# Weights cast by their own transfers from GpSimd's queue, in a kernel of chunked linear attention and a gated MLP

## The chip, the cores and the metric

The kernel runs on one core of a Trainium2 chip. The metric is the device time of one execution in microseconds (us); smaller is better. Times of before are the median of three runs.

A core has five engines that work side by side and meet at semaphores: TensorE (PE, matrix products; its weight loads are shown as PEld), VectorE (DVE), ScalarE (ACT), GpSimd (POOL) and SyncE (SP, which here only issues transfers). Data come from DRAM through 16 DMA engines into SBUF. Matrix products end in PSUM, here eight banks of 512 float32 a partition, used in pairs as tiles of two banks.

## The reference

A linear attention with a forget gate for every key channel runs over 768 steps, for 4 batches and 8 heads of 48 channels. Its output, as 3072 tokens of 384, goes through a layer whose activation is h times cos h.

```python
f = 1.0 / (1.0 + np.exp(-f_logit))
for t in range(S):
    state = f[:, :, t, :, None] * state + einsum('bhd,bhe->bhde', k[:, :, t], v[:, :, t])
    y[:, :, t] = einsum('bhd,bhde->bhe', q[:, :, t], state)
...
x = y.transpose(0, 2, 1, 3).reshape(B * S, H * D)
h = x @ w_in            # (3072, 384) @ (384, 2048)
g = h * np.cos(h)
out = g @ w_out         # (3072, 2048) @ (2048, 384)
```

All inputs and the output are float32. The kernel computes its products in bfloat16.

## The kernel before

**Tiling.** The sequence is cut into 24 chunks of 128 steps (4 batches of 6). Within a chunk the recurrence becomes matrix products: the logarithms of the gates are summed along the chunk by a product with a triangular matrix (`decay`), q and k are multiplied with the exponentials of these sums (the "qk" operations), scores are formed and masked ("sc", "am"), the state is moved on to the next chunk ("ps", "st", "sz" in `move_state`), and the chunk's output y is built from scores and state ("y"). It is turned into xT, tokens along the free axis, on PE or by a transposing transfer. The first 12 chunks are worked in pairs (`DUAL`, function `attend2`), in which a transfer reads two neighbouring rows of 192 bytes at once; the other 12 alone (`attend`).

**Decay.** `decay` runs for two chunks at a time: load f_logit, exp, ln, sum on PE, and two exponentials of the sum with either sign. Exp and ln use one ScalarE table, the cosine another; a change of table is a row ACT_TABLE_LOAD. Two such blocks make a group (`GROUPS`), whose exponentials stay together. `PR["gate"]` says for a group after how many cosines its first exponential may come. For the pairs in `HALVED` the loads of f, q and k, and the exponentials, are done in two halves of four heads, so that work can begin on the first.

**The MLP.** `moe` takes units of 128, 128 and then eleven times 256 tokens. A product h goes into a PSUM tile of two banks, each half from another stretch of w_in (L907, six products for 256 tokens, twelve for 128). ScalarE takes the cosine (L915), DVE multiplies (L924, into gT), and PE multiplies gT with w_out in four parts of four products for each 128 tokens (L934). One of DVE and ACT copies the result out (L513), and SP stores it (L942).

**Weights.** w_in and w_out are 3.1 MB each in float32. They come in four quarters each (`load_weights`). A quarter is 768 KB: SP's queue brings it as float32 into one of the six gT buffers, seen as float32, and then POOL, DVE or ACT casts it into `w_in_bf` or `w_out_bf` (L485). All products of L907 and L934 read from there.

**The order.** It is not written by hand. Every piece of work is entered in a planner (`Plan`) with its possible engines, their cost in ns, what it reads and writes, and a priority. `Plan.run` simulates the engines, picks at each step the operation that can start first (among those within `WINDOW`, that of the smallest priority), and thereby fixes the order of every engine's instructions and the buffers used. `PR` holds the priorities, `PIN` ties single operations to one engine. The planner's model of transfers is one bus: each takes its `dma` time after the one before it. `FETCH` belongs to a model of the instruction fetch of PE, and is 0 before. Where PE would stand still for long in the first 36 us of the plan, `keep_warm` puts in products with zeros (L448), whose results nobody reads.

**Dependencies inside a tile.** An operation that writes a whole `Val` waits for its last writer. A `Part` of a `Val` has writers of its own; a reader of the whole waits for all parts.

## Time and profile before

| what | value |
|---|---|
| median of 3 runs | 186.5 us (186.28 to 186.93) |
| profiled execution, its own time | 189.2 us |
| its span | 187.4 us |
| granted TensorE clock | 1.00 |
| products of w_in (L907), x624 | 67.9 us busy |
| products of w_out (L934), x400 | 68.9 us busy |
| cosines (L915, ACT), x48 | 53.4 us busy, 1113 ns each |
| gating products (L924, DVE), x48 | 60.1 us busy, 1265 ns each |
| casts of weights on POOL (L485), 4 | 1467 ns each |
| SP's queue, packets' time as a share of 16 engines' span | 78.4% |
| read from DRAM / written | 25.17 MB / 4.72 MB |

A row of instructions gives the line, engine, operation, output<-input by the program's names, shapes, count, busy time and the mean duration of one; behind the bar at the end stands the idle time of the engine just before them, and who ended it. In the slices of the span, each digit is a busy share in tenths. The chain of waits is followed back from the last instruction: each piece was released by the piece above it. "SPq" is time in which SP's queue issues a transfer, which is not the transfer itself. Times of a transfer "to landing" run from its issue until its data are there. PE's matmuls overlap, so that a row's mean (264 ns) is longer than the distance between two of them.

### The profile page before, as it was taken

The numbers are of one execution on the slowest core, as the hardware profiler recorded it, in microseconds if no ns is written. First come the engines' busy times: TensorE is split into PE (matmuls) and PEld (weight loads), VectorE is DVE, ScalarE is ACT, GpSimd is POOL, SyncE is SP. The second block draws the span as 40 slices with busy tenths as digits, with TensorE's granted clock in tenths as the row PEclk, the third lists the DMA queues.
The fourth block names the chain that finished last, engine by engine and source line by source line (L and its number), as shares of the span: only waits on it lengthen the run. The fifth ranks groups of instructions, "written<-read, shape, count | busy, mean of one in ns | idle before, by whom it ended". The sixth has DMA issues, their size and how long they took to land.

```text
span 187.4 us, 5205 instructions
## 1 busy us (share of the span) xinstructions
PE 177.6 (95%) x2169; PEld 129.9 (69%) x2169; DVE 130.3 (70%) x168; ACT 124.5 (66%) x156; POOL 69.6 (37%) x103
## 2 busy tenths in 40 slices
PE   6889789999989999999999999999999999999993
PEld 2456488767768785677776778876676976788663
DVE  5387888927669997538697577894588793477620
ACT  5585178897897599983779958699665720645401
POOL 8307274423544764431515724811681231000000
PEclk9999999999999999999999999999999999999999
DMA  5999999999999999999999989997884313111022
GB/s 140 272 259 315 379 380 348 229 235 302 251 181 215 245 181 204 190 240 186 184 218 189 128 220 189 222 199 138 203 170 82 63 25 84 42 45 42 2 85 84
DMA packets 99783, 34.51 MB, mean 184 GB/s; under 512 B 92976, under 2 KB 98224, under 8 KB 99760
## 3 DMA queue, kind: packets, MB, share of 16 engines
q1 hardware_dynamic: 99760, 34.19, 78.4%
q8 instruction: 17, 0.28, 0.7%
q14 instruction: 6, 0.05, 0.1%
HBM read 25.17 MB, written 4.72 MB: 159 GB/s over the span
## 4 chain that ended last, share of the span: by engine, by line
PE 68%; DMA 11%; SPq 8%; ACT 3%; POOL 3%; issue 3%; DVE 2%; DVEq 0%; POOLq 0%
PE ps L907 30%; PE ps L934 28%; SPq L499 6%; DMA gT<-in_moe_w_in_dram 6%; DMA ld<-in_q_dram 4%; SPq L479 2%; DMA xT<-yb 2%; POOL qk L642 2%; PE ps L831 2%; PE ps L863 1%; PE ps L569 1%; PE ps L859 1%; PE ps L845 1%; ACT f L537 1%; PE ps L626 1%
## 5 line engine op out<-in xcount | busy, mean ns | idle before, releaser
L924 DVE TENSOR_TENSOR gT<-ps,cosh 128x1024 bf16<-128x1024 f32 x48 | 60.1, 1265 | 16.7 <-ACT cosh L915 13.1
L915 ACT ACTIVATE cosh<-ps,halfpi 128x1024 bf16<-128x1024 f32 x48 | 53.4, 1113 | 24.4 <-PE ps L907 23.9
L907 PE MATMUL ps<-xT,w_in_bf 128*128 128x256 bf16 (+1 forms) x624 | 67.9, 264 | 1.5 <-DVE xT L513 0.4
L934 PE MATMUL ps<-w_out_bf,gT 128*128 128x384 bf16 (+2 forms) x400 | 68.9, 320 | 0.0
L907 PEld LDWEIGHTS <-w_in_bf 128*128 128x128 bf16 x624 | 56.1, 98 | 10.1 <-issue 1.7
L934 PEld LDWEIGHTS <-gT 128*128 128x128 bf16 x400 | 36.2, 98 | 20.3
L603 POOL TENSOR_TENSOR sz<-st,b 64x192 bf16<-64x192 f32 x32 | 16.8, 524 | 27.9 <-DVE st L596 24.9
L800 POOL TENSOR_TENSOR qk<-ld,b 128x384 bf16<-128x384 f32 x12 | 12.0, 1001 | 18.2 <-issue 6.4
L513 ACT COPY ot<-ps 128x384 f32<-128x384 f32 (+2 forms) x14 | 6.4, 454 | 17.7 <-PE ps L934 17.4
L835 DVE TENSOR_TENSOR am<-ps,umask 128x1024 bf16<-128x1024 f32 x12 | 14.5, 1216 | 3.7 <-PE ps L831 3.3
L698 DVE TENSOR_TENSOR am<-ps,pmask 128x1024 bf16<-128x1024 f32 x12 | 14.2, 1218 | 2.4 <-PE ps L693 1.9
L800 POOL TENSOR_TENSOR qk<-ld,bi 128x384 bf16<-128x384 f32 x12 | 11.9, 1002 | 6.2 <-DMA ld<-in_k_dram 6.1
L513 DVE COPY ot<-ps 128x384 f32<-128x384 f32 x11 | 6.1, 553 | 11.4 <-PE ps L934 11.4
L537 ACT ACTIVATE f<-f 128x768 f32<-128x768 f32 (+1 forms) x14 | 10.3, 748 | 3.6 <-DMA f<-in_f_logit_dram 3.6
L578 ACT ACTIVATE b<-ps 128x776 f32<-128x776 f32 (+1 forms) x14 | 10.1, 724 | 2.0 <-PE ps L566 1.6
L642 POOL TENSOR_TENSOR qk<-ld,b 128x384 bf16<-128x384 f32 x6 | 6.3, 1066 | 13.6 <-ACT b L578 11.7
L448 PE MATMUL ps<-zeros 128*128 128x512 bf16 x34 | 10.3, 430 | 1.0 <-DVE halfpi L375 1.0
L549 ACT ACTIVATE sp<-f 128x768 bf16<-128x768 f32 (+1 forms) x14 | 10.4, 751 | 0.3
L513 DVE CAST yb<-ps 128x384 bf16<-128x384 f32 x13 | 7.0, 552 | 4.7 <-PE ps L743 1.9
L578 ACT ACTIVATE bi<-ps 128x768 f32<-128x768 f32 (+1 forms) x14 | 10.1, 723 | 0.0
L513 ACT CAST yb<-ps 128x384 bf16<-128x384 f32 x9 | 4.3, 475 | 7.9 <-PE ps L743 6.1
L596 DVE TENSOR_TENSOR st<-ps,sz 128x384 f32<-128x384 f32 x16 | 8.8, 551 | 0.8 <-PE ps L845 0.7
(82 smaller groups left out, 177.3 us busy)
## 6 DMA issues: line engine op xcount, KB each, us to landing
out_dram<-ot SPq DMA_DIRECT2D x23, 192.0 KB, 2.8
f<-in_f_logit_dram SPq DMA_DIRECT2D x16, 192.0 KB, 4.3
ld<-in_q_dram SPq DMA_DIRECT2D x16, 192.0 KB, 4.3
ld<-in_k_dram SPq DMA_DIRECT2D x16, 192.0 KB, 3.8
gT<-in_moe_w_in_dram SPq DMA_DIRECT2D x4, 768.0 KB, 9.4
gT<-in_moe_w_out_dram SPq DMA_DIRECT2D x4, 768.0 KB, 11.5
ld<-in_v_dram SPq DMA_DIRECT2D x6, 384.0 KB, 5.7
ld<-in_v_dram SPq DMA_DIRECT2D x12, 192.0 KB, 3.7
```

What stands on the lines that cost most here:

```text
L499: P.op(nm + str(n), {"SP": 470.0}, lambda e, i=i, w=w, dst=dst: nc.sync.dma_start(out=(dst.ap if m == 2 else flat(dst.ap)).rearrange("p (h ...
L513: (nc.scalar.copy if e == "ACT" else nc.vector.tensor_copy)(out=o, in_=i_)
L537: first = P.op("exp", {"ACT": act(384 * w, "S")}, lambda e, s=s: nc.scalar.activation(out=flat(ft.ap[:, s]), in_=flat(ft.ap[:, s]), func=A ...
L578: nc.scalar.activation(out=out_.ap[:, s, :], in_=pc.ap.rearrange("p (m n) -> p m n", m=w)[:, :, 0:n], func=AF.Exp, scale=sign)
L603: eng().tensor_mul(out=like(S_out.ap, pv())[s, ..., r, :], in0=srcap()[s, ..., r, :], in1=d[..., None].broadcast_to(list(d.shape) + [D]))
L698: P.op("am", {"DVE": dve(1024)}, lambda e, sc=sc, am=am: nc.vector.tensor_mul(out=am.ap.rearrange("p r a n -> p (r a n)").rearrange("p (a ...
L800: P.op("qk", {"POOL": 1020.0}, lambda e, j=j, src=src, dec=dec: E(e).tensor_mul(out=qkv()[:, j, :, 0:D], in0=HB(src.ap), in1=HB(dec.ap[:, ...
L835: P.op("am", {"DVE": dve(1024)}, lambda e: nc.vector.tensor_mul(out=am.ap.rearrange("p r a n -> p (r a) n"), in0=sc.ap.rearrange("p (a n) ...
L907: nc.tensor.matmul(ph.ap[:, g * T:(g + 1) * T], lhsT=w_in_bf[:, f0 // 512, m, f0 % 512:f0 % 512 + 128], rhs=x[:, m, :], start=(g % (G // 2 ...
L915: nc.scalar.activation(out=co.ap, in_=ph.ap, func=AF.Sin, bias=halfpi),
L924: nc.vector.tensor_mul(out=o, in0=i0, in1=i1)
L934: nc.tensor.matmul(po.ap[:, 0:z - a], lhsT=gT.ap[:, j, i * C:(i + 1) * C], rhs=w_out_bf[:, j, a:z], start=(j == 0), stop=(j == KF - 1))
```

## The change

A quarter of the weights is now one transfer from GpSimd's queue, straight into `w_in_bf` or `w_out_bf`, which casts from float32 to bfloat16 on its way. The eight casts of L485 for weights are gone, and the stay in a gT buffer. In the planner such a transfer has a time before which it isn't placed (`hold`, in us, from `PR["wt"]`), costs 780 ns of POOL and reaches the bus 2400 ns later; the 800 ns that the planner added when the bus changed to weights are gone.

The two halves of a product h write parts of their tile, so that neither waits for the other in the plan. The four parts of an output product do the same, and whichever comes first in the order starts the sum in its bank, whichever comes last ends it.

The second pair of chunks (2 and 3) is no longer loaded and exponentiated in halves. `FETCH` is 6000 ns, the rule for filling products is a little wider, and the order is planned anew: all of `PR` and `PIN` are new values.

```diff
@@ -111,7 +111,7 @@
 
 class Op:
     __slots__ = ("seq", "eng", "fn", "prio", "table", "deps", "vals", "alloc", "start", "end",
-                 "lat", "waiting", "after", "grp", "dma", "name", "prior", "cost", "made", "form", "count")
+                 "lat", "waiting", "after", "grp", "dma", "name", "prior", "cost", "made", "form", "count", "hold")
 
 
 class Plan:
@@ -122,7 +122,7 @@
     FORM = 96.0
     WARM = 1000.0, 36000.0
     SPARE = 300.0
-    BLOCK, LEAD, FETCH = 256, 187, 0.0
+    BLOCK, LEAD, FETCH = 256, 187, 6000.0
     TABLE = 1290.0
     WINDOW = 120.0
 
@@ -130,12 +130,12 @@
         self.ops = []
 
     def op(self, name, eng, fn, reads=(), writes=(), prio=0.0, table=None, lat=0.0, grp=None,
-           dma=None, form=("full", "full"), count=0):
+           dma=None, form=("full", "full"), count=0, hold=0.0):
         o = Op()
         if PIN.get(len(self.ops)) in eng:
             eng = {PIN[len(self.ops)]: eng[PIN[len(self.ops)]]}
         o.name, o.eng, o.fn, o.prio, o.table = name, eng, fn, prio, table
-        o.lat, o.grp, o.dma, o.prior, o.form, o.count = lat, grp, dma, [], form, count
+        o.lat, o.grp, o.dma, o.prior, o.form, o.count, o.hold = lat, grp, dma, [], form, count, hold
         o.seq, o.deps, o.alloc, o.vals, o.after = len(self.ops), set(), [], [], []
         for v in reads:
             o.deps.update(v.writers)
@@ -161,7 +161,7 @@
     def run(self):
         free = {"PE": 0.0, "ACT": 800.0, "DVE": 3500.0, "POOL": 4500.0, "SP": 750.0}
         table, lock, bus, hot, pe_end, form, sent = None, None, 0.0, 0.0, 0.0, "full", []
-        warm, row = [], False
+        warm = []
         done, asked, due = 0, {}, self.LEAD
 
         def fetched(s, cost, count):
@@ -186,7 +186,7 @@
         while len(order) < n:
             cand = []
             for o in ready:
-                at, pe = 0.0, "PE" in o.eng
+                at, pe = o.hold * 1000.0, "PE" in o.eng
                 for d in o.deps:
                     t = d.end + (0.0 if pe and d.eng == "PE" else self.SEM)
                     if pe and d.eng == "PE":
@@ -239,8 +239,9 @@
                         for i in range(v.slot, v.slot + v.pool.size)}
                 idle = [(b["free"][i], i) for i in range(len(b["free"]))
                         if i in own - used or not (b["held"][i] or i in used)]
-                if idle and min(idle)[0] + 200.0 < t0:
-                    warm.append((o, t0, s - self.SPARE - t0, min(idle)[1]))
+                if idle and max(min(idle)[0] + 200.0, t0) + 300.0 < s - self.SPARE:
+                    at = max(min(idle)[0] + 200.0, t0)
+                    warm.append((o, at, s - self.SPARE - at, min(idle)[1]))
                 fetched(t0, s - self.SPARE - t0, int((s - self.SPARE - t0) / (427.0 if t0 < 3000.0 else 215.0)))
                 hot = 1.0 - (1.0 - hot) * math.exp((t0 - s + self.SPARE) / 2500.0)
                 pe_end = s - self.SPARE
@@ -254,14 +255,12 @@
             o.start = s
             free[e] = s + cost
             if o.dma is not None:
-
-                weights = o.name[0] == "w"
-                bus = max(s + cost + 700.0, bus) + o.dma + (800.0 if weights and not row else 0.0)
-                row = weights
+                bus = max(s + cost + (700.0 if e == "SP" else 2400.0), bus) + o.dma
                 o.end = bus + (1250.0 if len(sent) > 1 else 700.0)
-                sent.append(bus)
-                if len(sent) > 3:
-                    free[e] = max(free[e], sent[-4] + 900.0)
+                if e == "SP":
+                    sent.append(bus)
+                    if len(sent) > 3:
+                        free[e] = max(free[e], sent[-4] + 900.0)
             else:
                 o.end = s + cost + (self.PE_LAT if e == "PE" else 55.0 if e in ("ACT", "DVE") else 0.0)
                 o.lat = o.end - s - cost
@@ -308,44 +307,44 @@
 UNITS = [128, 128] + [256] * 11
 DUAL = [0, 2, 4, 6, 8, 10]
 FREE_GROUPS = 1
-HALVED = [0, 2]
+HALVED = [0]
 COLUMNS = [0]
 TURN_Y = range(14, 23)
 TURN_QK = range(10, 23)
 PR = {
 ...
-    "w_in": [-39.88, -40.08, -39.64, -38.03],
-    "w_out": [-34.2, -33.96, -37.04, -33.75],
-    "wc": [-70.63, -33.41, 50, 25.03, -16.34, 18.34, -16.44, -221.86],
-    "gate": [None, 2, 4, 12, 20, 24],
 ...
+    "w_in": [-12.77, -158.26, -81.6, -27.73],
+    "w_out": [121.95, 54.73, -17.25, 20.8],
+    "wt": [11.46, 10.76, 9.05, 9.22, 17.53, 16.94, 31.61, 12.85],
+    "gate": [None, 6, 4, 1, 18, 22],
 }
 ...
 
 
 def build(nc, cpool, ppool, q, k, v, f_logit, moe_w_in, moe_w_out, out):
@@ -464,22 +463,17 @@
     w_in_v = [Val(ap=w_in_bf[:, i] if nc is not None else None) for i in range(NW)]
     w_out_v = [Val(ap=w_out_bf[:, i * 4:(i + 1) * 4, :] if nc is not None else None) for i in range(NW)]
 
-    def load_weights(part, i, prio):
-
-        dst, stage = (w_in_v, w_out_v)[part][i], Val(gS)
-        w, cnt = ((512, KM), (d_model, 4))[part]
-        view = lambda: stage.ap.bitcast(F32).rearrange("p a n -> p (a n)")[:, 0:cnt * w].rearrange(
-            "p (a n) -> p a n", n=w)
+    def load_weights(part, i, prio, hold):
+
+        dst = (w_in_v, w_out_v)[part][i]
 
         def fn(e):
             if part == 0:
                 src = moe_w_in.rearrange("(km p) f -> p km f", p=128)[:, :, i * 512:(i + 1) * 512]
             else:
                 src = moe_w_out.rearrange("(kf p) m -> p kf m", p=128)[:, i * 4:(i + 1) * 4, :]
-            nc.sync.dma_start(out=view(), in_=src)
-        P.op(f"w{part}{i}", {"SP": 420.0}, fn, writes=[stage], prio=prio, dma=2130.0)
-        P.op("wc", {"POOL": 1480.0, "DVE": 920.0, "ACT": act(1536, "S")}, lambda e:
-             cast(e, dst.ap, view()), reads=[stage], writes=[dst], prio=PR["wc"][4 * part + i])
+            nc.gpsimd.dma_start(out=dst.ap, in_=src)
+        P.op(f"w{part}{i}", {"POOL": 780.0}, fn, writes=[dst], prio=prio, dma=2130.0, hold=hold)
 
     def cast(e, o, i_):
         (nc.scalar.copy if e == "ACT" else nc.vector.tensor_copy if e == "DVE" else nc.gpsimd.tensor_copy)(
@@ -909,7 +903,7 @@
                                              start=(g % (G // 2) == 0 and m == 0),
                                              stop=((g + 1) % (G // 2) == 0 and m == KM - 1))
                 P.op("h", {"PE": mm(T, 3 * G // 2)}, g1,
-                     reads=[xw] + [w_in_v[(j * G + half * G // 2) // 4]], writes=[ph], prio=pr,
+                     reads=[xw] + [w_in_v[(j * G + half * G // 2) // 4]], writes=[ph.part(None)], prio=pr,
                      count=3 * G // 2)
             cosines.append(P.op("cos", {"ACT": act(1024, ptr=True)}, lambda e, ph=ph, co=co:
                                 nc.scalar.activation(out=co.ap, in_=ph.ap, func=AF.Sin, bias=halfpi),
@@ -928,12 +922,15 @@
             pieces = [(0, d_model)] if r0 + C < n_tokens else [(0, 256), (256, d_model)]
             for a, z in pieces:
                 po, half = Val(p1S), ot.part(lambda o, a=a, z=z: o[:, a:z]) if len(pieces) > 1 else ot
+                told = []
                 for s in range(4):
-                    def g2(e, i=i, s=s, po=po, a=a, z=z):
+                    def g2(e, i=i, s=s, po=po, a=a, z=z, told=told):
+                        told.append(s)
                         for j in range(4 * s, 4 * s + 4):
                             nc.tensor.matmul(po.ap[:, 0:z - a], lhsT=gT.ap[:, j, i * C:(i + 1) * C],
-                                             rhs=w_out_bf[:, j, a:z], start=(j == 0), stop=(j == KF - 1))
-                    P.op("o", {"PE": mm(z - a, 4)}, g2, reads=[gT, w_out_v[s]], writes=[po], prio=pr + 0.001 * a,
+                                             rhs=w_out_bf[:, j, a:z], start=(len(told) == 1 and j == 4 * s),
+                                             stop=(len(told) == 4 and j == 4 * s + 3))
+                    P.op("o", {"PE": mm(z - a, 4)}, g2, reads=[gT, w_out_v[s]], writes=[po.part(None)], prio=pr + 0.001 * a,
                          count=4)
                 P.op("ot", {"ACT": act(z - a), "DVE": dve(z - a)}, lambda e, po=po, half=half, w=z - a: cp(
                     e, half.ap, po.ap[:, 0:w]), reads=[po], writes=[half], prio=pr)
@@ -945,9 +942,9 @@
 
     chunks = [(b, c) for b in range(B) for c in range(NCH)]
     for i in range(NW):
-        load_weights(0, i, PR["w_in"][i])
+        load_weights(0, i, PR["w_in"][i], PR["wt"][i])
     for i in range(NW):
-        load_weights(1, i, PR["w_out"][i])
+        load_weights(1, i, PR["w_out"][i], PR["wt"][4 + i])
     n, t0, units = 0, 0, list(UNITS)
     for g, group in enumerate(GROUPS):
         at0 = n
```

## The prediction

> **What bounds the kernel now.** I read the page's shares and slices first, then the busy time by stretches, then the same stretches for the filler matmuls of line 448 alone, then the chain of waits up to 62 us, and last the issue list of SP's queue. Page and stretches:
>
> ```profile
> span 187.4 us, 5205 instructions
> PE 177.6 (95%) x2169; PEld 129.9 (69%) x2169; DVE 130.3 (70%) x168; ACT 124.5 (66%) x156; POOL 69.6 (37%) x103
> ...
> DMA  5999999999999999999999989997884313111022
> ...
> 10.00:17.10 7.10, 6.54 (x177) 4.23 (x176) 6.45 (x10) 4.54 (x10) 2.45 (x3) 1.00 1.09 278
> 17.10:22.60 5.50, 4.20 (x87) 2.42 (x85) 4.28 (x7) 1.25 (x2) 2.26 (x5) 1.00 1.00 363
> 22.60:27.10 4.50, 4.03 (x67) 3.74 (x68) 3.44 (x6) 4.29 (x5) 3.16 (x3) 1.00 1.06 383
> 27.10:60.00 32.90, 32.02 (x450) 24.58 (x451) 24.43 (x29) 27.52 (x33) 13.17 (x14) 1.00 1.03 257
> 60.00:184.50 124.50, 123.24 (x1347) 91.26 (x1347) 86.92 (x101) 80.97 (x97) 43.15 (x58) 1.00 0.70 145
> ```
>
> The columns of a stretch are its length and then the busy time of PE, PEld, DVE, ACT, POOL, the granted clock, the DMA share and GB/s. TensorE is the bound: from 27.1 to 184.5 us it stands still for 0.88 + 1.26 = 2.1 us of 157.4, and after 184.5 there are 2.9 us of last eviction and store that nothing in the diff touches. What can be won lies ahead of 27.1, and a busy PE there is partly filler:
>
> ```profile
> L448 PE MATMUL ps<-zeros 128*128 128x512 bf16 x34 | 10.3, 430 | 1.0 <-DVE halfpi L375 1.0
> ...
> 0.00:10.00 10.00, 5.86 (x19) 1.94 (x19) 1.00 0.87 209
> 10.00:17.10 7.10, 2.16 (x8) 0.43 (x6) 1.00 1.09 278
> 17.10:22.60 5.50, 2.28 (x9) 0.76 (x9) 1.00 1.00 363
> ```
>
> Of the 5.5 us from 17.1 to 22.6, 1.30 are idle and 2.28 are filler: 3.58 us without useful work. From 22.6 to 27.1 another 0.47. Sum: 4.05 us. Before 17.1 there is more (8.0 of filler), but there the first chunks are still waiting for their own loads. The chain says what ends this:
>
> ```profile
> 13.27 1.69 SPq L479
> 14.96 0.04 issue
> 15.00 10.43 DMA gT<-in_moe_w_in_dram
> ...
> 25.55 1.48 POOL w_in_bf L485
> 27.03 0.05 issue
> 27.07 7.58 PE ps L907 x84
> 34.65 0.02 issue
> 34.68 1.11 ACT cosh L915
> 35.79 0.02 issue
> 35.81 1.28 ACT L1000
> ```
>
> The last quarter of w_in is issued at 15.00, lands at 25.43, is cast to bf16 on GpSimd for 1.48, and only then do 84 products run without a gap. After them come the cosine, the table load and the exponentials of the next chunks. The cast is on the path by name; the transfer ahead of it is the longer part.
>
> ```profile
> 11.25 4.98 SPq L479 DMA_DIRECT2D gT<-in_moe_w_in_dram  x4
> 16.27 7.64 SPq L479 DMA_DIRECT2D gT<-in_moe_w_out_dram  x4
> 23.96 5.92 SPq L499 DMA_DIRECT2D f<-in_f_logit_dram  x2
> ```
>
> For 12.6 us SP's queue issues nothing but weights. The forget gates of the third pair wait behind them until 23.96.
>
> **What the Trainium skill says.** "DMA: Bandwidth & Descriptors", section "SWDGE vs HWDGE vs iDMA": a transfer that changes the type has to come from GpSimd, whose cores compute its descriptors in software. No transfer in the trace of before is of that kind, so it shows no price. Same page, "Issuing engines are not separate DMA queues": transfers from different engines end on the same 16 DMA engines and interleave, and a second issuer saves only issue time. The trace agrees with the premise: the DMA share is 1.0 and more from 10 to 60 us, so there is no unused transfer time to fill. Same page, "Specifications": first byte about 1 us from GpSimd's path against about 0.6 us from SP's; not shown here, and small beside transfers that take 8 to 13 us to land. "PSUM — Partial Sum Buffer", "The four PSUM rules": the first matmul issued into a bank must be the one that starts the group, and groups in different banks do not disturb each other. That is what lets the two halves of a product swap; the trace cannot show it.
>
> **The change, part by part.**
>
> *Casts out.* Four of POOL at 1.467 us and, on DVE, three of 0.953 and one of 1.086: POOL loses 5.87 us, DVE 3.94. On the path is one of POOL's, 1.48 (25.55 to 27.03), with 0.12 of hand-over ahead of it: about 1.55 between landing and first product. The first product, at 22.58, waits likewise for a DVE cast of 0.95 that starts at 21.58. DVE's other casts run beside transfers that set the time. Staging buffers (gT) go too; no row waits for them, so I count nothing.
>
> *Issues moved from SP to POOL.* Eight at a cost the trace lacks. From below: SP's shortest weight issue is 0.52 us. From above: 1.5 us, about the price of the cast that each replaces. I take 0.8, near the 0.78 that the planner of the changed kernel is given: 8 x 0.8 = 6.4 us on POOL, 0.5 more than the casts gave back. POOL is busy 2.45 of 7.1 us from 10 to 17.1, so the w_in issues fit. Those of w_out that fall among the state updates (L603, at 17.3, 20.6 and 23.1) delay what is queued behind them: sz, the matmul of L735 that waited 1.27 us for it, and the third and fourth chunk's xT. Up to 0.8 us each; I put one, 0.8, on the path at worst, and zero as my value, since 27.1 and not 25.9 (the end of that xT) sets the long run of products.
>
> *SP's queue freed.* The forget gate of the third pair, the loads of k, q and v behind it can be issued from about 11.3 instead of 23.96, 12.6 us earlier, as far as buffers are free. They take transfer time from weights one for one. The gain is in the order only. Where it helps: at 44.83 the chain waits 7.19 us for a q load, with PE idle around it for 0.64 us (45 to 53 us).
>
> *Rate of the casting transfer.* 8 transfers of 768 KB. Before, two landings in a row are about 2.1 us apart, at 363 to 383 GB/s. The written bytes halve (w_in and w_out arrive as bf16), the read bytes don't. Lower bound: half, 1.05 us each, 8.6 us less DMA in all, if the write side were what limits; upper bound: twice, 4.3 us each, if the cast halves the rate. I take the same 2.1, because what is read from memory is unchanged.
>
> *When w_in lands.* With holds of 9.05 to 11.46 us in place of an issue at 11.25 to 15.00, the first bytes may go about 2 us earlier. The pair of loads that stand before them (q and v of the second pair, issued at 9.07 to 11.20) then share with them. All that is sent by then must still pass: at a full share in both kernels, the last w_in cannot be earlier by more than the bytes that now pass behind it. I take 1.0 us for this.
>
> *Free order of halves and of w_out quarters.* A product half no longer waits for the other half's weights, and the output product takes w_out quarters as they come. No row shows a wait by the order itself; it lets PE use whichever quarter landed first. Inside the 1.0.
>
> *Second pair unsplit; FETCH, filler rule, priorities and pins.* The second pair's loads and exponentials become one of 768 columns each instead of two of 384: four ACT rows of 748 instead of eight of about 500 save about 1 us of ACT, and delay the first half by one half-load, 0.75 us at 384 KB per 1.5 us. These cancel. The rest is the planner's own arithmetic and has no instruction. The new order could lose anywhere in the 157 us where PE is full; it holds at most the 2.1 us of idle time there as gain. I count zero.
>
> Sum: 1.55 + 1.0 = 2.55, say 2.5 us, inside the 4.05 that are there. The profiled execution took 189.2 (187.4 of span and 1.8 around it), so it would take 186.7. It was 2.7 above the median of the three timed runs; the same 2.5 off 186.5 gives 184.0.
>
> **The rivals.**
>
> *More is won (180.5 to 182.5, say 181.5).* All 4.05 us of the stretch to 27.1 become useful and the earlier loads of the third pair take out another 1 us around 45 to 53. For it: SP's 12.6 us. Against it: DMA is full all that time, so both cannot be early at once.
>
> *The gain is not kept (186.2).* PE starts 2.5 us earlier, runs out of work before the q load that lands at 52.02, and stands there. For it: between 45 and 60 PE waits for qk and for loads, its backlog is used up there. Against it: the issue of that q load hangs, through qk at 43.5, on the chain that begins at 27.07, so it moves too.
>
> *Slower (188.5).* One mechanism: at the 16 DMA engines weights from POOL's queue and loads from SP's take turns from about 11 us on. If w_in gets only half, its four transfers take 2 x 8.5 = 17 us in place of 8.5; begun at 12 they land at 29, against 27.03 for the end of the last cast before: 2 us more, 188.5. It decides from the point where the last w_in lands after 27.0. If instead weights take most of the turns (their pieces are 1.5 to 2 KB against 384 B), the second pair's q and v are late by as much, and xT of the third and fourth chunk with them. A cast at half rate has the same outcome and more: about +6, 192. For it: SP no longer stops for the weights, so loads do compete. Against it: loads are held by buffers (14 of ld, 3 of f).
>
> **How the numbers follow.** Forecast 0.42 (its own range 182.6 to 185.6); more 0.19; not kept 0.09, of which 0.07 within 0.3% and 0.02 just faster or slower; slower 0.30, of which 0.06 the slow cast. Faster by over 0.3% (below 185.9): 0.42 + 0.19 + 0.01 = 0.62. Within 0.3%, which is about what a measurement of this kernel can tell from no change: 0.07. Slower: 0.31. The range runs from 180.8, in the case of more, to 189.6, which takes in the sharing of queues with 1 us of POOL delay on top; the slow cast and the tail of the best case, under 0.2, are outside.
>
> **What would show it.** Right: products of L907 without a gap from 24 to 25 us on; less than 1.5 us of filler and idle time after 17 us; no casts of 128x1536; POOL rows of issue of about 0.8. Share: a last w_in landing after 27 and f landing much before 33. Not kept: an idle PE of 2 us and more between 40 and 60. A cast at half rate: landings of 4 us apart with nothing beside them. Wrong altogether: PE idle for more than 3 us between 60 and 184, from the new order.

## The result, and the profile after

Four runs of the changed kernel took 192.84 to 197.38 us, 193.23 in the median, against 186.4 (186.28 to 186.93) for the kernel before. The ratio is 1.035, with a 95% interval of 1.032 to 1.039: slower by 3.5%, outside the range and on the other side of the forecast. Some executions of any version take longer than the rest, here the one of 197.38 and the one of before that was profiled for the prediction (189.2), so medians are of all runs, ratios leave the longest out, and the profile of after (191.1 us of span, from a run of 192.84) is set beside a second one of the kernel before, called e0 here, with 185.9 us of span.

The page of after, its span and the busy shares, then two of its rows of slices in tenths:

```profile
span 191.1 us, 5172 instructions
...
PE 178.5 (93%) x2161; PEld 131.2 (69%) x2161; DVE 129.0 (68%) x161; ACT 123.9 (65%) x152; POOL 71.8 (38%) x110
...
PEclk9999969999999999999999999999999999999999
DMA  6999999999489985989999989997973202210122
```

PE is as busy as before (178.5 us; e0 has 178.0), so 4.7 of the 5.2 us more of span are time in which it stands; and part of its busy time is worth less, in one slice in which its clock is at 0.6. The largest part of the standing lies in the same place as that slice, as the stretches show (length, then PE, PEld, DVE, ACT, POOL, clock, DMA share, GB/s). First after, then e0:

```profile
17.10:22.60 5.50, 2.08 (x108) 1.43 (x109) 3.35 (x4) 2.29 (x2) 0.00 (x0) 1.00 1.21 208
22.60:27.10 4.50, 3.61 (x43) 3.35 (x43) 1.02 (x2) 0.07 (x1) 4.26 (x7) 0.62 1.21 241
...
60.00:185.00 125.00, 123.71 (x1352) 91.73 (x1353) 88.66 (x99) 87.16 (x104) 43.39 (x57) 1.00 0.71 143
```

```profile
17.10:22.60 5.50, 4.61 (x98) 3.11 (x97) 4.49 (x7) 1.69 (x3) 2.28 (x5) 1.00 1.05 386
22.60:27.10 4.50, 3.94 (x67) 3.63 (x64) 3.50 (x5) 3.37 (x5) 3.12 (x4) 1.00 1.08 375
```

From 17.1 to 27.1 us PE stands for 3.42 + 0.89 = 4.31 us in after and 0.89 + 0.56 = 1.45 in e0. That is 2.9 of the 4.7; another 1.2 lie before 17.1 us, and 0.7 after 27.1. POOL does nothing at all from 17.1 to 22.6. From 22.6 on PE's clock is 0.62 of full, which takes up to 0.38 x 4.5 = 1.7 us more. From 60 to 185 us it stands for 1.3 us of 125, so the new order shows no harm where PE is full. The chain of waits (start, length, what) says what POOL and PE wait for; first after, then e0:

```profile
9.01 13.55 DMA ld<-in_v_dram
...
22.61 0.83 POOL vb L479
...
23.49 0.83 PE ps L705 x16
24.32 2.67 PE ps L901 x24
...
30.55 7.40 PE ps L901 x84
37.95 4.55 PE ps L930 x28
```

```profile
13.02 11.50 DMA gT<-in_moe_w_in_dram
24.56 0.08 issue
24.64 1.48 POOL w_in_bf L485
26.12 0.05 issue
26.17 7.57 PE ps L907 x84
33.73 4.55 PE ps L934 x28
```

Not a weight but v of the second pair is late. It takes 13.55 us from issue to landing, POOL then casts it (vb), and the state product of L705 begins at 23.49. Behind it in PE's order stand the first products of w_in. The 24 of them take 2.67 us; at full clock e0 has 24 such in 1.51. The run of 84 products begins at 30.55 in place of 26.17, 4.4 of the 5.2 us; the other 0.8 arise after it and were not followed. PE's 4.31 - 1.45 = 2.9 us of longer standing and the 1.7 of clock make 4.6 beside these 4.4. The sum is rough: of e0's busy time from 17.1 to 27.1 us, 1.79 is filler, of after's 0.32.

Why v is late shows in the packets of the DMA queues: packets in the stretch, MB written, and their time as a share of 16 engines. SP's queue is q1, GpSimd's q0. After, from 17 to 19 us:

```profile
q0 software_dynamic: 307, 0.30, 88.3%
q1 hardware_dynamic: 306, 0.12, 32.7%
```

And e0, from 11 to 13 us, when only loads were moved:

```profile
DMA packets 1408, 0.53 MB, mean 263 GB/s; under 512 B 1408, under 2 KB 1408, under 8 KB 1408
...
q1 hardware_dynamic: 1408, 0.53, 127.6%
```

In after the two queues pass as many packets each, 306 against 307: they take turns by packet. A packet of a load has 0.12 MB / 306, about 384 bytes; one of w_in has 2 KB to read. Loads therefore move at 306 / 1408 = 22% of the speed that they have alone, while w_in takes nearly three quarters of the engines' time. In 2 us the engines pass 306 packets of all loads; v alone, 384 KB, has 1024 of them. Before, SP's queue was one line: q and v stood ahead of w_in and had all of the engines. By 13 us three of the four transfers of w_in had been issued in e0, and none of the 1408 packets is theirs, for all are under 512 B.

### The profile page after: what moved, and what is told of

Its sections match the earlier page's. It is cut to its first block, busy times and chain, and to the rows that moved or that the text cites. A ratio compares the mean times of both kernels' runs of the same rounds, so it can differ in the third digit from the quotient of the medians.

```text
span 191.1 us, 5172 instructions
## 1 busy us (share of the span) xinstructions
PE 178.5 (93%) x2161; PEld 131.2 (69%) x2161; DVE 129.0 (68%) x161; ACT 123.9 (65%) x152; POOL 71.8 (38%) x110
## 4 chain that ended last, share of the span: by engine, by line
PE 73%; DMA 11%; SPq 5%; ACT 4%; POOL 2%; DVE 2%; issue 1%; POOLq 0%; ACTq 0%
PE ps L901 32%; PE ps L930 29%; DMA ld<-in_v_dram 7%; SPq L493 4%; DMA qkt<-qk 3%; PE ps L825 2%; DMA f<-in_f_logit_dram 1%; PE ps L857 1%; POOL qk L794 1%; PE ps L620 1%; PE ps L563 1%; PE ps L839 1%; PE ps L853 1%; PE ps L687 1%; PE ps L705 1%
## 5 line engine op out<-in xcount | busy, mean ns | idle before, releaser
L901 PE MATMUL ps<-xT,w_in_bf 128*128 128x256 bf16 (+1 forms) x624 | 68.8, 268 | 0.1
L901 PEld LDWEIGHTS <-w_in_bf 128*128 128x128 bf16 x624 | 57.4, 100 | 8.5 <-issue 0.4
L597 POOL TENSOR_TENSOR sz<-st,b 64x192 bf16<-64x192 f32 x32 | 16.1, 503 | 32.3 <-DVE st L590 31.1
L636 POOL TENSOR_TENSOR qk<-ld,bi 128x384 bf16<-128x384 f32 x8 | 9.0, 1133 | 17.0 <-ACT bi L572 17.0
L794 POOL TENSOR_TENSOR qk<-ld,b 128x384 bf16<-128x384 f32 x12 | 12.0, 1001 | 6.4 <-DMA ld<-in_q_dram 4.1
L794 POOL TENSOR_TENSOR qk<-ld,bi 128x384 bf16<-128x384 f32 x12 | 11.9, 997 | 4.2 <-DMA ld<-in_k_dram 4.2
L479 POOL CAST vb<-ld 128x384 bf16<-128x384 f32 (+1 forms) x12 | 7.6, 641 | 15.3 <-DMA ld<-in_v_dram 10.3
L636 DVE TENSOR_TENSOR qk<-ld,b 128x384 bf16<-128x384 f32 x7 | 6.0, 876 | 10.1 <-ACT b L572 7.4
L636 POOL TENSOR_TENSOR qk<-ld,b 128x384 bf16<-128x384 f32 x5 | 5.6, 1133 | 10.8 <-ACT b L572 10.8
```

What stands on the lines that cost most here:

```text
L597: eng().tensor_mul(out=like(S_out.ap, pv())[s, ..., r, :], in0=srcap()[s, ..., r, :], in1=d[..., None].broadcast_to(list(d.shape) + [D]))
L636: P.op("qk", {"POOL": 1050.0, "DVE": 750.0}, lambda e, j=j, i=i, src=src, dec=dec: E(e).tensor_mul(out=parts[j][i].ap.rearrange("p e h d - ...
L794: P.op("qk", {"POOL": 1020.0}, lambda e, j=j, src=src, dec=dec: E(e).tensor_mul(out=qkv()[:, j, :, 0:D], in0=HB(src.ap), in1=HB(dec.ap[:, ...
L901: nc.tensor.matmul(ph.ap[:, g * T:(g + 1) * T], lhsT=w_in_bf[:, f0 // 512, m, f0 % 512:f0 % 512 + 128], rhs=x[:, m, :], start=(g % (G // 2 ...
```

## The experiments

All edits are to the kernel before or after, as named. `move(seqs, behind)` takes operations out of the finished order and puts them behind another one; nothing else of the order changes. Numbers of the order before: 0, 2, 4, 6 are the transfers of w_in, 8 to 14 those of w_out, 156 the first f load of the third pair, 104 the last qk of the second pair on POOL, 51, 117 and 120 the sz operations that end the three pairs of them, 7 the cast of the last quarter of w_in, 41 and 45 two "am" operations on DVE, ahead of which the memset of e14 to e16 stands. No kernel leaves out any of the computation; what is added is a cell or a few that nobody reads.

**e0: the kernel before again.**

> The kernel before, looked at once more, since its first profiled execution was 2.7 us above its own median. Every theory: about 186.4 us and a span of about 184.6; where it differs from the first profile tells where those 2.7 us were.

187.69 us, against a median of 187.78 of the same kernel in the runs beside it: 1.3 us above the 186.4 expected. It gave the profile used above. Part of what sets the first profile apart is in the weights: SP's queue passes 356 packets there from 17 to 19 us, and 396 in e0; the run of 84 products begins 0.9 us later (27.07, 26.17).

**e1: only the transfers cast; order, priorities and all else as before.**

```diff
-            nc.sync.dma_start(out=view(), in_=src)
+            nc.gpsimd.dma_start(out=dst.ap, in_=src)
...
-             cast(e, dst.ap, view()), reads=[stage], ...
+             None, reads=[stage], ...
```

> The kernel before with its own plan; only the eight weight transfers come from GpSimd's queue and cast, each at the place of its old issue, and the casts are gone. Theory A (weights and loads take turns packet by packet at the DMA engines, and the 384-byte packets of the loads lose): q and v of the second pair land late, PE stands at the state product of that pair, 3 to 7 us slower than before, 189 to 193 us. Theory B (the new plan is at fault, the casting transfer is sound): 1 to 2 us faster than before, about 185.

194.29 us, 1.032 [1.023, 1.041], against 1.035 for the whole change. The replanning, the free order of halves and quarters and the unsplit second pair together are worth nothing that these intervals show; the loss is in the transfers.

**e2 and e3: after, with w_in, and the first transfer of w_out, issued behind the cast of v on POOL; and after, with the first two products of w_in ahead of the state product on PE.**

```diff
+        move([2, 3, 1, 0, 7], 90)     # e2
+        move([52, 53], 97)            # e3
```

> The changed kernel; only the four issues of w_in and the first of w_out stand behind the cast of the second pair's v in POOL's order, so they can't start before that v has landed. Theory A: v lands at 14 to 17 instead of 22.6 us, the wait of 4.3 us at the state product goes, PE's clock stays full, w_in lands 4 to 6 us later than in the changed kernel (last one 28 to 31); 1 to 3 us faster than the changed kernel, 190 to 192. Theory B: within 0.5 us of the changed kernel or slower by as much as w_in is late, 193 to 197.

> The changed kernel; only the first two products h (24 matmuls, which need quarters 2 and 3 of w_in) stand ahead of the second pair's state product in PE's order. Theory A with the in-order wait as what costs: they run at about 19.4 us, inside the wait, 1.5 to 2.5 us of it are used and the matmuls after 23 us are less slow; 191 to 192. Theory B or a wait that something later sets again: within 0.5 us of the changed kernel, 193.

e2: 195.84 us, 1.044 [1.038, 1.050]. Now v is in time and w_in is late; the chain of e2 says so in three lines:

```profile
17.30 0.87 POOL w_in_bf L475
18.16 8.31 DMA w_in_bf<-in_moe_w_in_dram
...
32.62 7.40 PE ps L901 x84
```

The run begins at 32.62, later than the 30.55 of after. Theory A had w_in nearly as late as it came, but the time wrong, 190 to 192: PE now waits 3.70 and 1.20 us for w_in, which takes turns with loads in its place (313 packets to 311 from 24 to 26 us). e3: 195.1 us, 1.030 [1.021, 1.039], not told from after, where theory A had 191 to 192: the place of the first products in PE's order isn't it. Moving one party only chooses who is late.

**e4 and e5: e1 with order put back by hand.** A tiny store in SP's queue reads a cell of each quarter of w_in, so that later loads can't pass w_in (e4). In e5 a memset of one column a quarter also holds w_in back until the second pair's q is in, and its issues are spread over POOL.

```diff
+    P.fence = lambda: nc.sync.dma_start(out=fence, in_=w_in_bf[0:1, :, 0, 0:2])
+    P.hold = lambda: nc.vector.memset(w_in_bf[:, :, 0, 0:1], 0.0)      # e5 alone
...
+            if o.seq == 156:
+                P.fence()
```

> The kernel before with the casting transfers only (as e1_cast_only), and one tiny transfer on SP's queue, ahead of the third pair's forget gate, that waits until all four quarters of w_in are there: SP's later loads no longer run beside w_in. Theory A1 (w_in is late because loads that were not needed yet pass beside it): the last w_in lands 3 to 6 us earlier than in e1_cast_only, the long run of products starts earlier by as much; 188 to 191. Theory A2 (what costs is only that the second pair's q and v wait for w_in): within 1 us of e1_cast_only, 193 to 195.

> As e4_fence, and w_in isn't issued before the second pair's q has landed either (a small DVE write into w_in's buffer, which its transfers wait for, stands behind the product with that q), the four issues spread among POOL's work. Both directions of the sharing are gone then, nearly the order of transfers of the kernel before, without its casts. Theory A: the loss of e1_cast_only goes for the most part: within 1.5 us of the kernel before, 185 to 188. Theory C (casting transfers are slow or costly in themselves): still 3 us and more slower, 190 and more.

e4: 193.46, 1.032 [1.024, 1.040], the outcome of A2; v still lands at 21.7. e5: 190.87, 1.019 [1.014, 1.024]: two fifths of the loss gone, the clock at 1.0 throughout, the run of products from 29.14. What is left shows in its POOL and its transfers: the first w_in issue starts only at 14.51, and the DMA share from 10 to 17.1 us is 0.86, where e0 has 1.18. The order of loads and w_in is back, but the engines stand empty for a while. The time lies in the range of theory C, that casting transfers cost in themselves, and not in that of A; e5 can't refute C, e12 and e14 do.

**e6: e1 with every weight transfer cut in two by columns, so that a weight packet reads 1 KB.**

```diff
+            for c in range(2):
+                cut = slice(c * src.shape[-1] // 2, (c + 1) * src.shape[-1] // 2)
+                nc.gpsimd.dma_start(out=dst.ap[:, :, cut], in_=src[:, :, cut])
```

> As e1_cast_only, but every weight transfer is cut into two of half the columns, so that a packet of weights carries 1 KB or 768 bytes of float32 in place of 2 KB or 1.5 KB; the issues on POOL are 16. Turn-taking packet by packet: while both queues are busy, the loads get a larger share (34 against about 50 ns a turn, 40% in place of 27%), the second pair's v lands 3 to 5 us earlier than in e1_cast_only; the time as a whole is open, 190 to 196. Sharing by bytes or by transfers: v lands as in e1_cast_only.

If turns go by packet, smaller weight packets give loads more. From 16 to 18 us, e6:

```profile
q0 software_dynamic: 450, 0.22, 80.7%
q1 hardware_dynamic: 473, 0.18, 50.7%
```

Still about one to one, and 473 load packets where e4, with the same order up to there, has 291. v lands at 20.9 in place of 21.7, far less than the 3 to 5 us that were expected, and why so little was not followed. The time is no better, 194.36, 1.039 [1.031, 1.047]: w_in is slower for it, and POOL has 16 issues.

**e7: after, with e5's fence and hold.** In after's numbers, transfer 2 of w_in stands behind 89 and 3 behind 88 (qk operations of the second pair), 1 and 0 and the first transfer of w_out behind 90 (the cast of v), and SP's loads 150, 141, 149, 203 behind w_in.

> The changed kernel with both remedies: w_in held until the second pair's q has landed, and SP's loads from the third pair on behind the arrival of w_in. Theory A: most of the loss goes, 186 to 189. Theory B (the new plan costs of itself): 191 and more.

197.01, 1.051 [1.047, 1.055], the worst of all, in the range of theory B. PE is busy for only 12.46 of the 15 us from 45 to 60, and a cast of v on POOL waits until 37.35 for its load, so loads that are held too long are the likely reason; no run tests it. These remedies don't mend the new plan, and by itself this run would also fit a plan that costs something. Against that stands e1, which has the whole loss without the new plan.

**e8 and e9: w_out alone by casting transfers, w_in as before; and e5 with all of w_out later on POOL.**

```diff
+        move([8], 120); move([10, 12, 14], 7)      # e8
+        move([8, 10, 12, 14], 120)                 # e9, on e5
```

> The kernel before; w_in stays with SP's queue and its casts, only w_out's four transfers cast on their way, issued on GpSimd behind the second pair's state (one) and behind the last cast of w_in (three). Theory A: the second pair's loads and w_in are untouched, so the long run of products begins at 26 us as before; w_out's last quarter lands at 36 to 38, and PE waits up to 2 us for it: 186.5 to 189. Theory C (casting transfers cost wherever they stand): 190 and more.

> As e5_hold_fence, with the four issues of w_out behind the second pair's state updates on GpSimd instead of between them. Theory D (at 0.8 us each, issues lie on the path of the state on GpSimd): the third state update ends about 2 us earlier, the long run of products starts 1 to 2 us earlier, 189 to 190. If the arrival of w_in alone sets that run: as e5_hold_fence, 190.5 to 191.5.

e8: 193.36, 1.028 [1.022, 1.034]. The head is as before, and yet nearly the whole loss is there, again in theory C's range and not in A's. Two lines of its chain:

```profile
27.64 11.72 DMA w_out_bf<-in_moe_w_out_dram
...
39.40 5.28 PE ps L937 x16
```

Now it is the weight that is late: SP's loads, freed from waiting behind weights, are issued early and take every other turn (391 packets to 394 of w_out from 34 to 36 us). The 16 products of the last line take 5.28 us (e0 has 28 in 4.55): PE waits among them too, and its clock is 0.66 from 35 to 45 us. e9: 191.99, 1.026 [1.021, 1.030]. As theory D had it, the run begins 1.5 us earlier than in e5 (27.61 against 29.14), so there the issues did stand in the way of the state; but the time doesn't follow, because of e8's trouble behind the run: PE waits 1.60 us for w_out at 39.34.

**e10: the last cast of w_in on DVE in place of POOL, in the kernel before.** The cast is taken off the place where the prediction put 1.55 us.

```diff
+        [o for o in order if o.seq == 7][0].eng = "DVE"
```

> The kernel before; only the cast of w_in's last quarter is made by DVE (0.95 us) instead of GpSimd (1.47 us). If a cast on the chain counts one for one, as the prediction's first term takes it: 0.5 us faster, 0.3%, at the edge of what can be measured, and the long run begins 0.5 us earlier in the profile. If other waits take its place: no change.

187.47 against 187.3, 1.000 [0.996, 1.003]. PE's instructions (start, length; in brackets its idle time before and who ended it), e0 and then e10:

```profile
24.94 0.83 PE L907 MATMUL ps<-xT,w_in_bf 128*128 128x128 bf16 x12 [0.16 <-ACT xT L513]
26.17 7.57 PE L907 MATMUL ps<-xT,w_in_bf 128*128 128x128 bf16 x84 [0.40 <-POOL w_in_bf L485]
```

```profile
25.33 8.36 PE L907 MATMUL ps<-xT,w_in_bf 128*128 128x128 bf16 x96 [0.16 <-ACT xT L513]
```

The chain names the cast with 1.48 us, but PE had other products in the meantime and stood for only 0.40. That is all that its removal can bring where the other inputs come no earlier.

**e11 to e13: w_out alone casting, with a fence, and e10's edit.** e11 issues all four quarters behind 120 and lets SP's later loads wait for the third. e12 issues two of them 3 us earlier, in an idle stretch of POOL, and waits for the second; e13 waits for the first.

```diff
+    P.fence = lambda: nc.sync.dma_start(out=fence, in_=w_out_bf[0:1, 8, 0:2])   # e12: 4, e13: 0
...
+        move([8, 10, 12, 14], 120)                       # e11
+        move([8, 10], 117); move([12, 14], 120)          # e12, e13
```

> The kernel before with w_in as it was (SP's queue, float32, casts; the last cast on DVE instead of POOL), all four quarters of w_out by casting transfers from POOL, issued ahead of the place of e8_wout_only, and a tiny store in SP's queue ahead of the third pair's f, which waits for the third quarter of w_out to issue: what SP's single queue did for the order is put back by hand. Theory order (what costs is that weights and later loads take turns, not the cast itself): 186.5 to 188.5 us, against 193.4 of e8_wout_only, and no PE wait of over 0.5 us for w_out from 35 to 45 us. Theory cast (a casting transfer is itself slow, or takes POOL time that is on the path): 190 us or more, with w_out landing late although nothing of SP stands beside it.

> As e11_wout_fence, but two of the four w_out quarters are issued about 3 us earlier on POOL, in its idle stretch before the third pair of state operations, and the fence waits for the second quarter in place of the third. Theory order: the DMA engines have no hole from 22.5 to 25.5 us, the third pair's f is there before the table load ends at 36.2 us as in the kernel before, its v, q and k follow, and the time is 186.5 to 188.5 us. Theory cast: no hole, w_out in time, and still 190 us or more.

> As e12_wout_early with the fence behind the first quarter: the loads start about 2 us earlier and take turns with the last two quarters of w_out. Theory order: f, v and q land up to 1 us earlier than in e12_wout_early and w_out's last quarters 1 to 2 us later, but before the first output product needs them near 35 us; within 1 us of e12_wout_early. Theory cast: 190 us or more, as e12_wout_early.

e11 missed: 192.67, 1.029 [1.023, 1.034], where theory "order" had 186.5 to 188.5. But the outcome that theory "cast" named didn't come either: no product waits for w_out. One stretch of e11 shows what happened:

```profile
22.60:27.10 4.50, 3.98 (x68) 3.71 (x66) 3.80 (x6) 3.93 (x5) 4.42 (x6) 1.00 0.31 43
```

The DMA share is 0.31: w_in was through, w_out was issued from 24.0 on and sent its first packet after 25.6, and the fence kept everything else out. The experiment had put in a hole of its own, and f of the third pair came 1.6 us late. e12 closes it, and is the kernel before in time: 187.98 against 187.5, 1.002 [1.000, 1.004]; e13 1.003 [1.000, 1.005]. The same stretch in e12 has a DMA share of 1.21. For w_out, the casting transfer is not dear; the lost order was.

**e14: all eight transfers casting, each issued so that its packets begin when those before it end.** e1 with the hold released near 12 us and e12's fence.

```diff
+        move([2, 0], 41); move([4], 104); move([6], 51)
+        move([8, 10], 117); move([12, 14], 120)
```

> As e1_cast_only (order of the kernel before, all eight weight transfers casting), with each issue placed in POOL's idle stretches so that its packets begin as the ones before it end: two of w_in held by a tiny memset until near 12 us, the third near 16, the fourth near 18, two of w_out near 20.7 and two near 24, and SP's later loads behind a tiny store that waits for the second quarter of w_out. Theory order: v of the second pair lands by 17 us, the last of w_in by 25 us, the long run of products starts at 25 to 27 us, and the time is 186.5 to 189 us. Theory POOL (an issue delays the POOL work behind it, 0.78 us each, whatever the order): the third and fourth w_in issue push vb and sz back, the run starts at 28 us or later, 190 us or more.

187.94 against 187.39, 1.003 [1.000, 1.005]. Of the 3.2% of e1 nothing but 0.3% is left, by moves in POOL's order and one wait on either side. That refutes theory POOL. POOL in e14:

```profile
12.24 1.71 POOL L482 DMA_DIRECT2D w_in_bf<-in_moe_w_in_dram  x2 [4.16 <-DVE w_in_bf L453]
...
15.89 0.80 POOL L482 DMA_DIRECT2D w_in_bf<-in_moe_w_in_dram  x1
16.69 0.83 POOL L488 CAST vb<-ld 128x768 bf16<-128x768 f32 x1
...
18.52 0.81 POOL L482 DMA_DIRECT2D w_in_bf<-in_moe_w_in_dram  x1
```

v is cast at 16.69, where after has 22.61. And a third of the gain that the prediction hoped for is there, and is given back. PE in e14:

```profile
24.72 8.17 PE L910 MATMUL ps<-xT,w_in_bf 128*128 128x128 bf16 x96 [0.24 <-ACT xT L516]
...
51.41 0.62 PE L680 MATMUL ps<-ident,qk 128*128 128x128 bf16 x8 [0.86 <-DVE qk L645]
```

The 96 products end at 32.90, 0.83 us before those of e0 (33.73); in e15, below, they end 0.80 before. At 51 us PE waits 0.86 us for a qk, where e0 waits for nothing. In e14's chain the step ahead of it is a load of q that takes 7.12 us, from 43.65 to 50.77. In e0 the same load is issued at 43.23, and the qk on POOL that waits for it starts at 49.34.

**e15 and e16: can it be kept?** e15 is e14 with the fence on the first quarter of w_out; e16 also issues the first w_in about 1 us earlier, and moves the memset with it.

```diff
-    P.fence = lambda: nc.sync.dma_start(out=fence, in_=w_out_bf[0:1, 4, 0:2])
+    P.fence = lambda: nc.sync.dma_start(out=fence, in_=w_out_bf[0:1, 0, 0:2])
...
-        move([2, 0], 41)
+        move([2, 0], 45)      # e16
```

> As e14_all_in_order with SP's later loads behind the first quarter of w_out in place of the second. The transfers had a thin stretch near 30 to 32 us in e14, before the loads came; it goes, at the price of turns with w_out's last quarters. If that hole is what gave the earlier products back at 45 to 60 us: PE idle there falls from 1.25 us to under 0.7 and the time is 0.3 to 0.8 us below e14. If the loads only take from w_out: w_out's last quarter lands after 34 us and the time is that of e14 or up to 1 us more.

> As e15_fence_first with the first two w_in issues about 1 us earlier (held until near 11 us), so that their packets begin before the last loads end. If the hole near 14 us mattered, 0.3 us less than e15; if turns with q and v of the second pair matter at once, v lands about 1 us later and the time is 0 to 1 us more than e15.

No. e15: 188.13 against 187.81, 1.001 [0.999, 1.003]; PE stands for 1.31 us from 45 to 60, as in e14 (1.25), so the thin stretch near 30 us was not what gave the time back. e16: 1.004 [1.001, 1.007], not told from e15. No version was found that is faster than the kernel before.

## Why the prediction was wrong

The step that failed is "SP's queue freed", where loads "take transfer time from weights one for one. The gain is in the order only." It was counted as costing nothing; e1 puts it at 3.2%, 6 us. That the engines were full was right: from 17.1 to 22.6 us the DMA share is above 1 in both kernels. But the order was not a gain to be had; it was what the kernel before owned, and the change gave it up. SP's single queue sent loads and weights in the order of issue (from 11 to 13 us in e0 not one packet of the w_in that was already issued); the two queues take turns by packet (306 to 307). In the prediction this stood as the rival "Slower", with 0.30. Its first branch had w_in late by 2 us, and its sign, a last w_in landing after 27, did not come (24.6); its second had q and v late "by as much", because weights have the larger packets. The second is what happened, but with 6.5 us for v (vb at 22.61 against 16.12 in e0) and not 2, since packets of unequal size in equal turns leave the loads 22% and not a half. The 4.3 us for which PE then stood also cost it clock, a term that the prediction didn't have. Shown by e1 (the transfers alone do it), by e2 (the other party late), by e6 (turns by packet), and by e12 and e14 (order back, time back).

The other terms of the sum:

- *Casts out, 1.55:* the mechanism is there and the size wrong, at most 0.40 (e10). The chain of waits gives the length of a piece, not what would be gained without it. PE's own idle time gives that: in the first profile it stood 0.31 us ahead of the 84 products and, against what the prediction says, not at all ahead of the products at 22.58. The 0.47 us of idle time from 22.6 to 27.1 that the prediction itself lists is less than a third of this term.
- *w_in lands 1.0 earlier:* zero in after. Its last quarter was issued near 11.4 (the row below) and took 13.2 us, so it landed at 24.6; the chain of e0 has 24.5. In e14 the products end 0.83 earlier, casts and landing together, in place of 2.55.
- *Issues on POOL, 0.8 each:* right in price. The row of w_in's issues in after (least, median and most ns), and the times from issue to landing of its four transfers:

```profile
L475 POOL DMA_DIRECT2D w_in_bf<-in_moe_w_in_dram x4: 772/775/931, 8.9 to 11.4; - x4
...
DMA to landing us min/median/max: 6.4/9.9/13.2
```

They were off the path, as valued: POOL had nothing else to do while v was missing. Where v is in time they can be on it: from e5 to e9 the run begins 1.5 us earlier with the issues of w_out moved behind the state updates.

- *Rate of the casting transfer, 2.1 us a quarter:* right. With the engines to itself GpSimd's queue passes 399 packets of w_in in 2 us (e14, 18 to 20 us), SP's queue 387 to 396 (e0, 15 to 21 us).
- *Free order, unsplit pair, new plan, 0 together:* e1 against the result leaves them near zero. They were not tried one by one, and e7 leaves room for a cost of the plan.
- *Not kept (186.2):* this rival's mechanism is what e14 shows. Its argument against, that the late q load "moves too", was wrong: PE is earlier by 0.83 us and waits 0.86 for it, and the load comes more than 1 us later than in e0.

The Trainium skill bears on both halves. "DMA: Bandwidth & Descriptors", "Issuing engines are not separate DMA queues", says that transfers from different engines interleave and that a second issuer saves only issue time. The prediction took from it that there is no transfer time to win; what interleaving itself can cost, it left to a rival, and the runs show 3%. "TensorE: Matmul & The Clock Gate", part 1, says that the clock is low by default and activity releases it. The trace agrees: 0.62 after a stop of 4.3 us, 1.00 in the same stretch of e14, where PE hardly stops (0.36 us from 17.1 to 22.6).

What stays open: the load of q at 43.65 in e14 that keeps the 0.8 us from arriving. e15 rules out the thin stretch near 30 us as its cause; the load is issued 0.4 us later than in e0 and then takes about 1 us longer, and what holds it back wasn't tried. Nor was the new plan run with transfers in e14's order; e7 is the only try, so what that plan is worth by itself is open.

## What to carry to other kernels

Where transfers are full, a single queue is a schedule: before moving a stream to another engine's queue, ask what stood behind what, and count the packets, because here each queue got its turns by packet and the one with the small packets lost. If the stream has to move, keep the order by hand, with a small write that holds its start and a small read that fences what follows, and see that neither leaves the engines empty. And price a step by the idle time of the bounding engine just before it, not by its length in the chain.

## What was not expected of the hardware

- Equal turns by packet between two queues: 306 against 307 in 2 us with packets of 384 B and 2 KB, 473 against 450 with 384 B and 1 KB. It isn't so in every stretch: in e8, from 28 to 30 us, loads pass 638 packets and w_out 337, and no run shows why.
- A casting transfer is as fast as a plain one when it has the engines for itself: in e14, from 18 to 20 us, 399 packets, against 387 to 396 in 2 us for w_in from SP's queue in e0, a few of them small in both.
- From the start of its issue on GpSimd to its first packet a casting transfer took about 1.6 us with nothing in its way (e11: issue at 24.0, none before 25.6). In e11 a hole followed (DMA share 0.31); in e12, with two transfers issued ahead, there is none (1.21).
- Taking eight casts, 9.8 us of busy time, away from POOL and DVE brought no time: e14 has none of them, and is at 1.003. PE is the engine that bounds.
